# Last batch of an attention and gated-MLP kernel in chunks of 424, 424 and 240 columns, its gates in other buffers, and its keys in three stretches of matmuls per batch

## The chip, the cores and the metric

The kernel runs on one core of a Trainium2 chip. The core has a matmul engine (TensorE, in the profile PE, with the loads of its stationary operand listed apart as PEld), VectorE (DVE), ScalarE (ACT), GpSimd (POOL) and SyncE (SP), which issues the DMAs. Each engine works through its own list of instructions in order and waits on semaphores for the others. The metric is the time of one execution on the device in microseconds: the median of three runs of this kernel is 345.65 us (345.07 to 345.81).

## The reference

For each of four batches, linear attention with features that are outer products of two small projections, and then a gated MLP that mixes over the sequence:

```python
# q, k, v: (4, 4 heads, 1088, 32); S1, S2: (8, 32)
phi(x) = outer(S1 x, S2 x)                       # 64 features per head
kv = sum_s phi(k)_s v_s ;  z = sum_s phi(k)_s
x  = (phi(q) kv) / (phi(q) z + 1e-6)             # (4, 1088, 128)
h  = relu(x @ w_in)                              # (4, 1088, 1024)
u, v = h[..., :512], h[..., 512:]
v_n = (v - mean(v)) / sqrt(var(v) + 1e-6)
v_s = w_spatial @ v_n + b_spatial                # 1088 x 1088 over the sequence
out = (u * v_s) @ w_out                          # (4, 1088, 128)
```

The weights come in float64. The kernel splits them, and what it multiplies them with, into a high and a low fp32r part, and replaces a product by three (high by high, low by high, high by low).

## The kernel before, in words

A batch b has two halves. `attention(b)` makes x: queries, keys (`keys`), their products, and then `hidden_v`, which gives the normalised v half. `main(b)` does the rest with the sequence on the free axis. Its work is cut into blocks (d, c): d counts the four groups of 128 of the 512 hidden units, c the chunks of the 1088 output positions, which the table `CH` sets to 364, 362 and 362 columns. A block has

- `hidden(d, c)`: three matmuls (lines 357 to 359) into the bank `pu`, and a Relu on ACT (line 867) into a tile u,
- `spatial`: 26 matmuls over the nine pieces kt of the sequence into a bank `sp` (lines 875, 877, 884, 886),
- `gate`: DVE multiplies `sp` by u (line 913), ACT casts the product to its high part (line 437), DVE subtracts to get the low part (line 367),
- `out_mm`: three matmuls with w_out into a bank `po`, which collects over d. They are held back by one block in the list `late`.

After the last d a copy takes `po` to SBUF and a DMA takes it out. In the last batch the last block is cut in two, of 182 and 180 columns, and the sums of its chunk lie in two banks (`po` and `sd`) for all four d, so that each d there has six short out matmuls in place of three. One half is copied by DVE (line 857), the rest by ACT (line 855).

Tiles come from small rings: u from three buffers, which also serve the copies `ob`, the gates' parts from three buffers g (for the last d also r), attention's feature tiles from eight buffers pl, x in its parts from two buffers each, xh and xl.

Nobody writes the instructions' order down. Every step is recorded by `op` with an engine, a cost and a due time, and `Order.schedule` then walks through a modelled time: of what can start it takes what is due first, and fixes each engine's list and each tile's buffer. A changed cost or tile therefore can move instructions elsewhere.

In `keys(b)` for b over 0, three pieces g of the sequence are projected (`project`, 6 small matmuls a piece, line 531) and summed with v (`part`, 12 small matmuls a piece, line 579); the trace has two records for each of these. Here the matmuls are plain fp32 and 64 wide, and they stand in stretches between the fp32r matmuls of `main(b - 1)`: first the projection of piece 0, then twice a projection with the sums of the piece before, then the sums of the last piece.

Of the kernel before, what the change touches and what calls it, by code (L numbers as in the profile page):

```python
# [19 lines left out]
P = 128  # L20
# [5 lines left out]
CH = [(0, 364, 0), (364, 362, 1), (726, 362, 2), (726, 182, 2), (908, 180, 2)]  # L26
# [275 lines left out]
def c_dve(n):  # L302
    return 152 + 1.045 * n
# [10 lines left out]
def c_mm(n, k=1):  # L314
    return k * (n + 10.3) / 2.25
# [3 lines left out]
def tile_kernel(ctx: ExitStack, tc: tile.TileContext, kT, qT, vA, sks, idn, msk, wT, w_in, w_out, bsp, out):  # L319
# [166 lines left out]
    def load_w(kt, c):  # L486
        c0, cw, _ = CH[c]
# [36 lines left out]
    def ab_view(ab):  # L524
        return ab[:, :192].rearrange("p (x t c) -> p x t c", t=3, x=2)

    def project(ab, xt):

        for t in range(3):
            for j in range(2):  # L530
                nc.tensor.matmul(ab_view(ab)[64 * j:64 * j + 64, :, t], xt[:, t * P + 64 * j:t * P + 64 * j + 64], sk[:, :NSK], start=True, stop=True)  # L531

    def features(b, g, ab, what):

        a_sb = tl("ka", f"{what}a{b}{g}", [P, 3, 32])
        op("ACT", c_act(96, True), lambda: nc.scalar.copy(out=a_sb.ap, in_=ab_view(ab)[:, 0]), r=[ab], w=[a_sb])
        f = tl("kp", f"{what}p{b}{g}", [P, 3, H * R * R])
        if not b:
            op("DVE", c_dve(768), lambda: nc.vector.tensor_tensor(
                out=f.ap.rearrange("p t (h i j) -> p (t h) i j", h=H, i=R),  # L540
                in0=a_sb.ap.rearrange("p t (h i) -> p (t h) i", h=H).unsqueeze(3).broadcast_to([P, 12, R, R]),
                in1=ab_view(ab)[:, 1].rearrange("p t (h j) -> p (t h) j", h=H).unsqueeze(2).broadcast_to([P, 12, R, R]),
                op=ALU.mult,
            ), r=[a_sb, ab], w=[f])
            return f
        for a in range(2):
            op("DVE", c_dve(384), lambda a=a: nc.vector.tensor_tensor(
                out=f.ap.rearrange("p t (r i a j) -> p (t r) i a j", r=2, i=R, a=2)[:, :, :, a],
                in0=a_sb.ap.rearrange("p t (r a i) -> p (t r) a i", r=2, a=2)[:, :, a].unsqueeze(3).broadcast_to([P, 6, R, R]),
                in1=ab_view(ab)[:, 1].rearrange("p t (r a j) -> p (t r) a j", r=2, a=2)[:, :, a].unsqueeze(2).broadcast_to([P, 6, R, R]),  # L550
                op=ALU.mult,
            ), r=[a_sb, ab], w=[(f, a)])
        return f
# [6 lines left out]
    def keys(b):  # L560
# [9 lines left out]
        f = phi(b, 0, xts[0], "k")  # L570
# [13 lines left out]
        for g in range(3):  # L584
            if b and g < 2:

                ab = bank("sd", f"kab{b}{g + 1}")
                op("PE", 1510, lambda g=g, f=f, ab=ab: (project(ab, xts[g + 1]), part(g, f)), r=[f, vs[g], xts[g + 1], (sk, "x")], w=[kv, ab])
                f = features(b, g + 1, ab, "k")
            else:  # L590
                op("PE", 950, lambda g=g, f=f: part(g, f), r=[f, vs[g]], w=[kv])
                if g < 2:
                    f = phi(b, g + 1, xts[g + 1], "k")
# [174 lines left out]
    def main(b, st):  # L768
        po = [None] * 5
# [67 lines left out]
        def out_mm(d, c, gh, gl):  # L837
            c0, cw, _ = CH[c]
            if b == B - 1 and c == 2:

                for part in (3, 4):
                    out_part(d, part, gh, gl, CH[part][0] - c0)
            else:
                out_part(d, c, gh, gl, 0)

        def out_part(d, c, gh, gl, g0):
            c0, cw, _ = CH[c]
            if d == 0:
                po[c] = bank("sd" if c == 4 else "po", f"po{b}{c}")
            o = po[c]  # L850
            op("PE", c_mm(cw, 3), lambda: mm3(o[:, :cw], woh[:, d], wol[:, d], gh[:, g0:g0 + cw], gl[:, g0:g0 + cw], start=(d == 0), stop=(d == ND - 1)), r=[gh, gl, (woh, d // 2), (wol, d // 2)], w=[o], due=due(c_mm(cw, 3)))
            if d == ND - 1:
                ob = tl("u", f"ob{b}{c}", [P, CW])
                if c != 4:
                    op("ACT", c_act(cw, True), lambda: nc.scalar.copy(out=ob[:, :cw], in_=o[:, :cw]), r=[o], w=[ob], due=clock[0] + 8000)
                else:
                    op("DVE", c_dve(cw), lambda: nc.vector.tensor_copy(out=ob[:, :cw], in_=o[:, :cw]), r=[o], w=[ob], due=clock[0] + 8000)
                op("SP", 470, lambda: nc.sync.dma_start(out=out[b, :, c0:c0 + cw], in_=ob[:, :cw]), r=[ob], kb=181, due=clock[0] + 12000)

        def hidden(d, c, tag="pu"):  # L860
            c0, cw, _ = CH[c]
# [4 lines left out]
            u = tl("u", f"u{b}{d}{c}", [P, CW])  # L866
            op("ACT", c_act(cw, True), lambda: nc.scalar.activation(u[:, :cw], pu[:, :cw], AF.Relu), r=[pu], w=[u], lead=LEAD[0])  # L867
            return u

        def high(d, c, sp, kt):  # L870

            vh, vl, vx = hl[d]
            c0, cw, _ = CH[c]
# [35 lines left out]
        def gate(d, c, sp, u):  # L909
            cw = CH[c][1]  # L910
            tag = "r" if last(d) and c < 2 else "g"
            gh, gl = tl(tag, f"gh{b}{d}{c}", [P, CW], F32R), tl(tag, f"gl{b}{d}{c}", [P, CW], F32R)
            op("DVE", c_dve(cw), lambda: nc.vector.tensor_tensor(out=u[:, :cw], in0=sp[:, :cw], in1=u[:, :cw], op=ALU.mult), r=[sp], w=[u], lead=LEAD[1])  # L913
            split(lambda: gh[:, :cw], lambda: gl[:, :cw], lambda: u[:, :cw], cw, [u], [gh], [gl])
            return gh, gl
# [120 lines left out]
```

## Time and profile before

| | |
|---|---|
| median of three runs | 345.65 us |
| the profiled execution | 345.83 us, of which the profile's span is 344.1 us |
| PE busy | 336.0 us, 98% of the span |
| PEld, DVE, ACT, POOL busy | 323.0, 208.2, 160.0, 52.5 us |
| granted TensorE clock | 1.00 of 2.4 GHz over the whole span |
| chain of waits | PE 87%, DVE 5%, DMA 4% of the span |

Matmuls are pipelined: one starts long before the one ahead has ended, so their busy times overlap. What one costs in a row of them is the distance of two starts. The time between the span and the execution's own time, 345.83 less 344.1, is 1.73 us.

### The profile page before, as it was taken

How to read it: one execution, taken by the hardware profiler on the slowest of the kernel's cores; microseconds unless marked ns; L12 is line 12 of the kernel's file. 1: busy time of each engine (PE TensorE's matmuls, PEld its weight loads, DVE VectorE, ACT ScalarE, POOL GpSimd, SP SyncE). 2: the span in 40 equal slices, each digit the busy share in tenths (PEclk: the TensorE clock that was granted, in tenths of full speed). 3: DMA queues.
4: the chain of work that ended last, by engine and by line, in shares of the span. 5: the costliest groups of instructions: out<-in, count | busy, mean ns of one | idle time of the engine just before them, and what ended most of it. 6: DMA issues, size and time to landing. Idle time of an engine off the chain costs nothing.

```text
span 344.1 us, 6204 instructions
## 1 busy us (share of the span) xinstructions
PE 336.0 (98%) x2363; PEld 323.0 (94%) x2363; DVE 208.2 (61%) x480; ACT 160.0 (47%) x369; POOL 52.5 (15%) x66
## 2 busy tenths in 40 slices
PE   7889999999999999999999999999999999999995
PEld 7878999999999999999999999999999999999994
DVE  4799999833789993558995045235499941212122
ACT  2479746733667662445673153125666532112122
POOL 1030100352322034501300024302200000000000
PEclk9999999999999999999999999999999999999999
DMA  6556036865510056611000056400000010000001
GB/s 214 161 171 202 2 86 167 264 115 111 159 39 27 2 105 108 159 54 46 21 0 2 22 92 137 79 0 3 0 0 2 22 45 0 0 2 0 2 2 65
DMA packets 18502, 23.10 MB, mean 67 GB/s; under 512 B 2856, under 2 KB 17960, under 8 KB 18472
## 3 DMA queue, kind: packets, MB, share of 16 engines
q1 hardware_dynamic: 18472, 22.71, 26.0%
q8 instruction: 18, 0.29, 0.4%
q14 instruction: 12, 0.10, 0.1%
HBM read 13.78 MB, written 2.23 MB: 47 GB/s over the span
## 4 chain that ended last, share of the span: by engine, by line
PE 87%; DVE 5%; DMA 4%; ACT 1%; SPq 1%; issue 1%; DVEq 0%; ACTq 0%
PE sp L875 21%; PE sp L884 18%; PE sp L877 18%; PE sd L358 3%; PE sd L359 3%; PE sd L357 3%; PE pu L357 2%; PE pu L359 2%; PE pu L358 2%; PE sp L886 2%; PE po L357 2%; PE po L358 2%; PE po L359 2%; PE sd L579 2%; DMA c<-in_qT 1%; PE sd L531 1%
## 5 line engine op out<-in xcount | busy, mean ns | idle before, releaser
L875 PE MATMUL sp<-wTh,vh 128*128 128x362 f32 (+3 forms) x423 | 139.9, 331 | 0.0
L877 PE MATMUL sp<-wTh,vl 128*128 128x362 f32 (+3 forms) x376 | 122.6, 326 | 0.1
L884 PE MATMUL sp<-wTl,vh 128*128 128x362 f32 (+3 forms) x376 | 120.5, 326 | 0.0
L875 PEld LDWEIGHTS sp<-wTh,vh 128*128 128x128 f32 x423 | 79.6, 188 | 1.3
L877 PEld LDWEIGHTS sp<-wTh,vl 128*128 128x128 f32 x376 | 70.8, 188 | 1.0 <-DVE vl L824 0.6
L884 PEld LDWEIGHTS sp<-wTl,vh 128*128 128x128 f32 x376 | 70.8, 189 | 0.0
L913 DVE TENSOR_TENSOR u<-sp,u 128x362 f32<-128x362 f32 (+3 forms) x47 | 24.5, 523 | 71.9 <-PE sp L886 66.7
L437 ACT CAST g<-u 128x362 fp32r<-128x362 f32 (+3 forms) x47 | 23.0, 489 | 60.2 <-DVE u L913 60.2
L867 ACT ACTIVATE u<-pu 128x362 f32<-128x362 f32 (+3 forms) x49 | 22.9, 467 | 26.5 <-PE pu L359 26.2
L367 DVE TENSOR_TENSOR g<-u,g 128x362 fp32r<-128x362 f32 (+3 forms) x47 | 26.7, 569 | 13.3 <-ACT g L437 12.0
L740 DVE BATCH_NORM_STATS2 st<-vt 128x6 f32<-128x512 f32 x36 | 24.2, 686 | 9.1 <-ACT vt L738 8.9
L738 ACT ACTIVATE vt<-sd 128x512 f32<-128x512 f32 x36 | 21.3, 596 | 13.3 <-PE sd L359 12.6
L718 DVE RECIPROCAL c<-c 128x384 f32<-128x384 f32 (+1 forms) x9 | 21.8, 2418 | 8.1 <-ACT c L716 6.8
L370 POOL TENSOR_TENSOR r<-pl,r 128x384 fp32r<-128x384 f32 (+1 forms) x18 | 17.3, 969 | 43.6 <-ACT r L437 43.6
L687 POOL TENSOR_TENSOR pl<-pl,pl 128x384 f32<-128x384 f32 (+1 forms) x18 | 17.7, 982 | 36.1 <-DMA pl<-abT 26.4
L793 ACT CAST vh<-vt 128x384 fp32r<-128x384 f32 x36 | 17.8, 512 | 9.0 <-DVE vt L760 7.5
L370 POOL TENSOR_TENSOR r<-c,r 128x384 fp32r<-128x384 f32 (+1 forms) x9 | 9.4, 1061 | 77.8 <-ACT r L437 77.8
L795 DVE TENSOR_TENSOR vl<-vt,vh 128x384 fp32r<-128x384 f32 (+1 forms) x36 | 17.3, 504 | 0.8 <-ACT vh L793 0.6
L357 PE MATMUL pu<-xh,wih 128*128 128x362 f32 (+3 forms) x49 | 16.2, 331 | 0.0
L359 PE MATMUL pu<-xh,wil 128*128 128x362 f32 (+3 forms) x49 | 16.0, 327 | 0.0
L358 PE MATMUL pu<-xl,wih 128*128 128x362 f32 (+3 forms) x49 | 15.9, 324 | 0.0
L760 DVE TENSOR_SCALAR vt<-vt,mv,sm 128x512 f32<-128x512 f32 x31 | 15.5, 540 | 0.0
(147 smaller groups left out, 526.4 us busy)
## 6 DMA issues: line engine op xcount, KB each, us to landing
pl<-in_wT SPq DMA_DIRECT2D x18, 181.0 KB, 2.9
v<-in_vA SPq DMA_DIRECT2D x12, 198.0 KB, 4.0
kt<-in_kT SPq DMA_DIRECT2D x12, 192.0 KB, 3.8
pl<-abT SPq DMA_DIRECT2D x12, 192.0 KB, 4.0
c<-in_qT SPq DMA_DIRECT2D x9, 192.0 KB, 3.2
pl<-abT SPq DMA_DIRECT2D x24, 72.0 KB, 2.6
pl<-in_wT SPq DMA_DIRECT2D x9, 182.0 KB, 2.6
out<-u SPq DMA_DIRECT2D x7, 181.0 KB, 2.6
```

Of the source, the lines that this page charges most:

```text
L357: nc.tensor.matmul(o, ah, bh, start=start, stop=False)
L358: nc.tensor.matmul(o, ah, bl, start=False, stop=False)
L359: nc.tensor.matmul(o, al, bh, start=False, stop=stop)
L367: return lambda: nc.vector.tensor_tensor(out=o(), in0=a(), in1=bb(), op=ALU.subtract)
L370: return lambda: nc.gpsimd.tensor_tensor(out=o(), in0=a(), in1=bb(), op=ALU.subtract)
L437: op("ACT", c_act(n), lambda: nc.scalar.copy(out=hi(), in_=x()), r=r, w=wh)
L740: op("DVE", 690, lambda stats=stats, t=t: nc.vector.bn_stats(out=stats.ap, in_=vt[:, t]), r=[(vt, t)], w=[stats])
L867: op("ACT", c_act(cw, True), lambda: nc.scalar.activation(u[:, :cw], pu[:, :cw], AF.Relu), r=[pu], w=[u], lead=LEAD[0])
L875: nc.tensor.matmul(sp[:, :cw], vh[:, kt], wTh[:, kt, cs], start=(kt == 0), stop=False)
L877: nc.tensor.matmul(sp[:, :cw], vl[:, kt], wTh[:, kt, cs], start=False, stop=False)
L884: nc.tensor.matmul(sp[:, :cw], vh[:, kt], wTl[:, kt, cs], start=False, stop=False)
L913: op("DVE", c_dve(cw), lambda: nc.vector.tensor_tensor(out=u[:, :cw], in0=sp[:, :cw], in1=u[:, :cw], op=ALU.mult), r=[sp], w=[u], lead=LEA ...
```

## The change

Three things, all in the order of PE or at the end.

1. In the last batch the chunks are 424, 424 and 240 columns (`CH_LAST`), and no block is cut in two. The wide chunks take u and the copies `ob` from the ring pl, and both gate parts of chunk 0 share one buffer of the ring xh, of chunk 1 one of xl; each ring has one buffer to spare there, since the other holds the batch's x. In the last d the held-back out matmuls all come after the last block.
2. The last chunk's `po` is copied by halves, DVE the second and ACT the first.
3. `keys` of batches 1 to 3 projects pieces 0 and 1 together, then piece 2 with the sums of piece 0, and then sums pieces 1 and 2.

```diff
+CH_LAST = [(0, 424), (424, 424), (848, 240)]
...
-        for g in range(3):
-            if b and g < 2:
-                ab = bank("sd", f"kab{b}{g + 1}")
-                op("PE", 1510, lambda g=g, f=f, ab=ab: (project(ab, xts[g + 1]), part(g, f)), r=[f, vs[g], xts[g + 1], (sk, "x")], w=[kv, ab])
-                f = features(b, g + 1, ab, "k")
-            else:
...
+        ab = bank("sd", f"kab{b}0")
+        op("PE", 950, lambda ab=ab: (project(ab, xts[0]), project(ab, xts[1], 192)), r=[xts[0], xts[1], (sk, "x")], w=[ab])
+        f0, f1 = features(b, 0, ab, "k"), features(b, 1, ab, "k", 192)
+        ab = bank("sd", f"kab{b}2")
+        op("PE", 1305, lambda ab=ab: (project(ab, xts[2]), part(0, f0)), r=[f0, vs[0], xts[2], (sk, "x")], w=[kv, ab])
+        f2 = features(b, 2, ab, "k")
+        op("PE", 1660, lambda: (part(1, f1), part(2, f2)), r=[f1, f2, vs[1], vs[2]], w=[kv])
...
-                for part in (3, 4):
-                    out_part(d, part, gh, gl, CH[part][0] - c0)
...
-                ob = tl("u", f"ob{b}{c}", [P, CW])
-                if c != 4:
-                    op("ACT", c_act(cw, True), lambda: nc.scalar.copy(out=ob[:, :cw], in_=o[:, :cw]), r=[o], w=[ob], due=clock[0] + 8000)
-                else:
-                    op("DVE", c_dve(cw), lambda: nc.vector.tensor_copy(out=ob[:, :cw], in_=o[:, :cw]), r=[o], w=[ob], due=clock[0] + 8000)
+                ob = tl("pl" if wide else "u", f"ob{b}{c}", [P, cw])
+                n = cw
+                if wide and c == 2:
+                    n = cw // 2
+                    op("DVE", c_dve(n), lambda: nc.vector.tensor_copy(out=ob[:, n:], in_=o[:, n:cw]), r=[o], w=[(ob, 1)], due=clock[0] + 8000)
+                op("ACT", c_act(n, True), lambda: nc.scalar.copy(out=ob[:, :n], in_=o[:, :n]), r=[o], w=[(ob, 0)], due=clock[0] + 8000)
...
+            u = tl("pl" if wide and c < 2 else "u", f"u{b}{d}{c}", [P, cw])
...
-            tag = "r" if last(d) and c < 2 else "g"
+            if wide and c < 2:
+                g = tl(("xh", "xl")[c], f"g{b}{d}{c}", [P, 2, cw], F32R)
+                parts = [(lambda: g[:, 0], (g, 0)), (lambda: g[:, 1], (g, 1))]
+            else:
+                tag = "r" if last(d) else "g"
...
-            if late and not (last(d) and c):
+            if late and not last(d):
                 out_mm(*late.pop(0))
...
-        if b == B - 1:
-            blocks[-1:] = [(ND - 1, 3), (ND - 1, 4)]
```

The first place is PE's list in batch 1's keys, at the last of their stretches, before; `kp` holds features, `sd_117` the sums, `sp` the mixing of batch 0.

```order
L875 MATMUL sp_290<-wTh,vh 128x362
L877 MATMUL sp_290<-wTh,vl 128x362
L884 MATMUL sp_290<-wTl,vh 128x362
L579 MATMUL sd_117<-v_113,kp_134 64x66 x12
L875 MATMUL sp_290<-wTh,vh 128x362
L877 MATMUL sp_290<-wTh,vl 128x362
```

The same place of PE's list after the change, where lines are shifted by one or so.

```order
L876 MATMUL sp_290<-wTh,vl 128x362
L883 MATMUL sp_290<-wTl,vh 128x362
L579 MATMUL sd_117<-v_109,kp_138 64x66 x12
L579 MATMUL sd_117<-v_113,kp_134 64x66 x12
L874 MATMUL sp_290<-wTh,vh 128x362
L876 MATMUL sp_290<-wTh,vl 128x362
```

The sums of piece 1 (`kp_138`), which stood behind a projection twelve rows earlier, now stand beside those of piece 2, and the projection of piece 1 stands beside that of piece 0 in the same way; a stretch is gone.

The second place is the end of PE's list before: the out matmuls behind the last matmul of the last block, with the semaphores that each waits for.

```order
L886 MATMUL sp_252<-wTl,v_85 128x180
L357 MATMUL po_266<-r_788,woh 128x364
L358 MATMUL po_266<-r_800,woh 128x364
L359 MATMUL po_266<-r_788,wol 128x364
L357 MATMUL po_115<-r_776,woh 128x362 [waits Activation_49]
L358 MATMUL po_115<-r_786,woh 128x362 [waits DVE_49]
L359 MATMUL po_115<-r_776,wol 128x362
L357 MATMUL po_237<-g_674,woh 128x182 [waits Activation_49]
L358 MATMUL po_237<-g_640,woh 128x182 [waits DVE_49]
L359 MATMUL po_237<-g_674,wol 128x182
L357 MATMUL sd_117<-g_650,woh 128x180 [waits Activation_49]
L358 MATMUL sd_117<-g_640,woh 128x180 [waits DVE_49]
```

The same after the change, from the first out matmul behind the last block (whose last matmul has 240 columns) to the end of the list.

```order
L358 MATMUL po_237<-g_650,woh 128x240
L359 MATMUL po_237<-g_640,woh 128x240
L360 MATMUL po_237<-g_650,wol 128x240
L358 MATMUL po_266<-xh_309,woh 128x424
L359 MATMUL po_266<-xh_309,woh 128x424 [waits DVE_49]
L360 MATMUL po_266<-xh_309,wol 128x424
L358 MATMUL po_115<-xl_319,woh 128x424 [waits Activation_49]
L359 MATMUL po_115<-xl_319,woh 128x424 [waits DVE_49]
L360 MATMUL po_115<-xl_319,wol 128x424
L358 MATMUL po_237<-r_788,woh 128x240 [waits Activation_49]
L359 MATMUL po_237<-r_800,woh 128x240 [waits DVE_49]
L360 MATMUL po_237<-r_788,wol 128x240
```

Twelve out matmuls follow the last block in both, but now the first three are the third group's on the last chunk (`g_650`, `g_640`), the next six are wide, and the last two parts (`r_788`, `r_800`) have buffers of their own, while before the last low part went into `g_640`, which the three matmuls ahead of it read.

The third place is the end of ACT's list before.

```order
L437 CAST g_650<-u_679 128x180 [waits DVE_49]
L855 COPY u_609<-po_266 128x364 [waits PE_49,Activation_49]
L855 COPY u_635<-po_115 128x362 [waits PE_49,Activation_49]
L855 COPY u_679<-po_237 128x182 [waits DVE_49,PE_49]
L1032 UNCONDITIONAL_BRANCH
```

And after the change; DVE's last row there is its own copy of the other half of `po_237`, which waits for PE.

```order
L438 CAST r_788<-u_635 128x240 [waits DVE_49]
L856 COPY pl_191<-po_266 128x424 [waits PE_49]
L856 COPY pl_63<-po_115 128x424 [waits PE_49]
L856 COPY pl_212<-po_237 128x120 [waits DVE_49]
L1036 UNCONDITIONAL_BRANCH
```

The last copy on ACT now waits for DVE alone and not for PE, that is for DVE's copy of the other half of the same bank; no copy waits for a DMA any more, since the buffers pl are free.

## Rows read from the trace of the kernel before

**Rows 1.** The page: busy time by engine, and the granted clock in 40 slices.
```profile
PE 336.0 (98%) x2363; PEld 323.0 (94%) x2363; DVE 208.2 (61%) x480; ACT 160.0 (47%) x369; POOL 52.5 (15%) x66
PEclk9999999999999999999999999999999999999999
```

**Rows 2.** Windows, last batch: PE, PEld, DVE, ACT, POOL busy, clock, DMA.
```profile
280.00:325.00 45.00, 45.00 (x276) 45.00 (x276) 9.13 (x17) 8.62 (x18) 0.00 (x0) 1.00 0.01 5
```

**Rows 3.** Waits of PE from 40 us to the end: total, times, longest.
```profile
PE sd L358 <- DVE g L367: 0.3, 1, 0.3
```

**Rows 4.** Timeline of PE (start, us, ...): 26 of 364 columns, 6 of 512.
```profile
289.32 0.33 PE L357 MATMUL pu<-xh,wih 128*128 128x364 f32 x1
...
293.65 0.25 PE L357 MATMUL po<-g,woh 128*128 128x182 f32 x1
...
242.41 0.40 PE L357 MATMUL sd<-wih,xh 128*128 128x512 f32 x1
...
243.81 0.33 PE L875 MATMUL sp<-wTh,vh 128*128 128x362 f32 x1
```

**Rows 5.** Timeline of PE: 182 columns behind wide ones, 16 steps of 180.
```profile
325.99 0.25 PE L357 MATMUL po<-g,woh 128*128 128x182 f32 x1
326.07 0.28 PE L358 MATMUL po<-g,woh 128*128 128x182 f32 x1
...
336.02 0.27 PE L875 MATMUL sp<-wTh,vh 128*128 128x180 f32 x1
...
337.81 0.27 PE L886 MATMUL sp<-wTl,v 66*128 66x180 f32 x1
```

**Rows 6.** Groups of DVE and ACT from 325 us on: busy us, mean ns, idle before.
```profile
L913 DVE TENSOR_TENSOR u<-sp,u 128x364 f32<-128x364 f32 x1 | 0.5, 536 | 4.0 <-PE sp L886 4.0
...
L437 ACT CAST r<-u 128x364 fp32r<-128x364 f32 x1 | 0.5, 497 | 4.4 <-DVE u L913 4.4
...
L855 ACT COPY u<-po 128x364 f32<-128x364 f32 x1 | 0.5, 455 | 0.0
...
L855 ACT COPY u<-po 128x182 f32<-128x182 f32 x1 | 0.3, 311 | 0.2 <-DVE g L367 0.2
```

**Rows 7.** Timeline of PE: last matmul ahead, second behind, three stretches of batch 3.
```profile
204.97 0.33 PE L359 MATMUL pu<-xh,wil 128*128 128x362 f32 x1
...
205.99 0.33 PE L877 MATMUL sp<-wTh,vl 128*128 128x362 f32 x1
...
209.70 0.32 PE L884 MATMUL sp<-wTl,vh 128*128 128x362 f32 x1
...
211.43 0.33 PE L877 MATMUL sp<-wTh,vl 128*128 128x362 f32 x1
...
222.62 0.32 PE L884 MATMUL sp<-wTl,vh 128*128 128x362 f32 x1
...
224.00 0.32 PE L877 MATMUL sp<-wTh,vl 128*128 128x362 f32 x1
```

**Rows 8.** Line 547, products of features: ns min/median/max, first and last start.
```profile
L547 DVE TENSOR_TENSOR kp<-ka,sd x18: 541/548/556, 67.0 to 216.0; 128x384 f32<-128x384 f32 x18
```

**Rows 9.** Timeline behind the last block; in brackets idle time before, releaser.
```profile
338.12 0.35 DVE L913 TENSOR_TENSOR u<-sp,u 128x180 f32<-128x180 f32 x1 [1.12 <-PE sp L886]
...
338.50 0.34 ACT L437 CAST g<-u 128x180 fp32r<-128x180 f32 x1 [1.88 <-DVE u L913]
...
339.41 0.35 DVE L367 TENSOR_TENSOR g<-u,g 128x180 fp32r<-128x180 f32 x1 [0.94 <-PE po L359]
...
340.00 0.27 PE L359 MATMUL sd<-g,wol 128*128 128x180 f32 x1
341.22 0.35 DVE L857 COPY u<-sd 128x180 f32<-128x180 f32 x1 [1.46 <-DMA out<-u]
```

**Rows 10.** DMA issues by size: KB each, median us from issue to landing.
```profile
out<-u SPq DMA_DIRECT2D x4, 182.0 KB, 1.9
...
out<-u SPq DMA_DIRECT2D x1, 91.0 KB, 1.9
```

More of the change, by code (lines that the diff above doesn't have):

```diff
@@ L486, in load_w @@
     def load_w(kt, c):
-        c0, cw, _ = CH[c]
+        c0, cw = CH[c]
         cs = slice(c0, c0 + cw)
@@ L521, in load_sq, with ab_view, project, features @@
         split(lambda: sqh.ap, lambda: sql.ap, lambda: sq[:, :P], P, [sq], [sqh], [sql])
-    def ab_view(ab):
-        return ab[:, :192].rearrange("p (x t c) -> p x t c", t=3, x=2)
-    def project(ab, xt):
+    def ab_view(ab, at=0):
+        return ab[:, at:at + 192].rearrange("p (x t c) -> p x t c", t=3, x=2)
+    def project(ab, xt, at=0):
         for t in range(3):
             for j in range(2):
-                nc.tensor.matmul(ab_view(ab)[64 * j:64 * j + 64, :, t], xt[:, t * P + 64 * j:t * P + 64 * j + 64], sk[:, :NSK], start=True, stop=True)
-    def features(b, g, ab, what):
+                nc.tensor.matmul(ab_view(ab, at)[64 * j:64 * j + 64, :, t], xt[:, t * P + 64 * j:t * P + 64 * j + 64], sk[:, :NSK], start=True, stop=True)
+    def features(b, g, ab, what, at=0):
         a_sb = tl("ka", f"{what}a{b}{g}", [P, 3, 32])
-        op("ACT", c_act(96, True), lambda: nc.scalar.copy(out=a_sb.ap, in_=ab_view(ab)[:, 0]), r=[ab], w=[a_sb])
+        op("ACT", c_act(96, True), lambda: nc.scalar.copy(out=a_sb.ap, in_=ab_view(ab, at)[:, 0]), r=[ab], w=[a_sb])
         f = tl("kp", f"{what}p{b}{g}", [P, 3, H * R * R])
@@ L582, in part @@
                         )
[L584 to L593 removed]
+        if not b:
+            for g in range(3):
+                f = phi(b, g, xts[g], "k")
+                op("PE", 950, lambda g=g, f=f: part(g, f), r=[f, vs[g]], w=[kv])
+            return kv
+        ab = bank("sd", f"kab{b}0")
[5 more added lines that the diff above has]
+        op("PE", 1660, lambda: (part(1, f1), part(2, f2)), r=[f1, f2, vs[1], vs[2]], w=[kv])
         return kv
@@ L768, in main @@
     def main(b, st):
-        po = [None] * 5
+        po = [None] * 3
+        cols = CH_LAST if b == B - 1 else CH
+        wide = b == B - 1
         clock, rate = [T_MAIN[b] * 1e3], [1.0]
@@ L835, in split_t, with out_mm @@
                 op("DVE", c_dve(DH), low9(nc.vector), r=[(vt, t)], w=[(h, kt) for h in hs], sh=True, alts=[("POOL", c_pool(DH), low9(nc.gpsimd))], kind="vl0")
[L837 to L847 removed]
+        def out_mm(d, c, hi, lo, parts):
+            c0, cw = cols[c]
@@ L848, in out_part @@
             if d == 0:
-                po[c] = bank("sd" if c == 4 else "po", f"po{b}{c}")
+                po[c] = bank("po", f"po{b}{c}")
             o = po[c]
-            op("PE", c_mm(cw, 3), lambda: mm3(o[:, :cw], woh[:, d], wol[:, d], gh[:, g0:g0 + cw], gl[:, g0:g0 + cw], start=(d == 0), stop=(d == ND - 1)), r=[gh, gl, (woh, d // 2), (wol, d // 2)], w=[o], due=due(c_mm(cw, 3)))
+            op("PE", c_mm(cw, 3), lambda: mm3(o[:, :cw], woh[:, d], wol[:, d], hi(), lo(), start=(d == 0), stop=(d == ND - 1)), r=[*parts, (woh, d // 2), (wol, d // 2)], w=[o], due=due(c_mm(cw, 3)))
@@ new lines, in out_mm @@
+                n = cw
[3 more added lines that the diff above has]
+                op("ACT", c_act(n, True), lambda: nc.scalar.copy(out=ob[:, :n], in_=o[:, :n]), r=[o], w=[(ob, 0)], due=clock[0] + 8000)
+                op("SP", 470, lambda: nc.sync.dma_start(out=out[b, :, c0:c0 + cw], in_=ob.ap), r=[ob], kb=cw // 2, due=clock[0] + 12000)
@@ L889, in spatial @@
             vh, vl, vx = hl[d]
-            _, cw, wc = CH[c]
+            c0, cw = cols[c]
+            wcs = [n for n, (w0, w) in enumerate(CH) if w0 < c0 + cw and c0 < w0 + w]
             g = kt // 3
@@ L895, in spatial @@
             if high in parts:
-                r += ([(vl, key)] if kt < NK else []) + [(wTh, (kt, wc))]
+                r += ([(vl, key)] if kt < NK else []) + [(wTh, (kt, wc)) for wc in wcs]
             if low in parts:
-                r += [(wTl, (kt, wc))] + ([(wTl, ("bias", 0)), (wTl, ("bias", 1)), vx] if kt == NK else [])
+                r += [(wTl, (kt, wc)) for wc in wcs] + ([(wTl, ("bias", 0)), (wTl, ("bias", 1)), vx] if kt == NK else [])
             def f():
@@ L909, in gate @@
         def gate(d, c, sp, u):
-            cw = CH[c][1]
-            tag = "r" if last(d) and c < 2 else "g"
[L912 to L915, printed above, removed]
+            cw = cols[c][1]
+            op("DVE", c_dve(cw), lambda: nc.vector.tensor_tensor(out=u.ap, in0=sp[:, :cw], in1=u.ap, op=ALU.mult), r=[sp], w=[u], lead=LEAD[1])
+            if wide and c < 2:
[3 more added lines that the diff above has]
+                tag = "r" if last(d) else "g"
+                gh, gl = tl(tag, f"gh{b}{d}{c}", [P, cw], F32R), tl(tag, f"gl{b}{d}{c}", [P, cw], F32R)
+                parts = [(lambda: gh.ap, gh), (lambda: gl.ap, gl)]
+            (hi, wh), (lo, wl) = parts
+            split(hi, lo, lambda: u.ap, cw, [u], [wh], [wl])
+            return hi, lo, [wh, wl]
         late = []
```

20 lines of the change are left out of this document (8 added, 12 removed).

## The prediction

> **What bounds the kernel now.** I read the page first: TensorE is busy for 98% of the span, at a granted clock of 1.00 throughout (the 2.4 GHz level), and no other engine above 61% [rows 1]. Then the busy time by stretches: in the last batch TensorE is busy for all 45.00 us of the window from 280 to 325 us, its weight loads too [rows 2]. Then TensorE's waits: behind the first 40 us there is one, of 0.3 us, at the very end [rows 3]. So the time is the sum of TensorE's steps plus what follows its last one, and it is no use to look at the other engines before the end. A busy time of overlapping matmuls says nothing of their price, so the timeline gives that as distances of starts. 26 matmuls of 364 columns take 293.65 - 289.32 = 4.33 us, 0.1665 each; six of 512 take 1.40 us, 0.2333 each [rows 4]. In a row of short ones, 16 steps of 180 columns take 1.79 us, 0.112 each; but the one 182-column step that follows wide matmuls takes 0.08 [rows 5]. So 182 columns stream in 0.08, and a row of them is held at 0.112 by something else; every matmul has a weight load of its own, 276 of each in that window [rows 2], so I take the loads as that floor.
>
> **Last batch: 41 matmuls fewer.** Up to the last matmul of the last block (the tail behind it comes below) the last batch had 125 matmuls of 364 and 212 of 362 columns and 76 short ones: twelve blocks of 29, the last one done twice on halves, and three out matmuls per block (six on the cut chunk) less the twelve of the tail. At 0.1665 and 0.112 that is 56.11 + 8.51 = 64.62 us. Now it is 250 of 424 and 122 of 240. The trace has neither width. For 424 I go along the line between 364 and 512 columns, 0.00045 us a column: 0.1665 + 60 x 0.00045 = 0.1936; the two rows also bound it, at 0.1665 and 0.2333, but a line through them has held at both. For 240 the same line gives 0.111 and the floor of the short ones 0.112; the far bounds are the 0.08 of a lone short step and the 0.1665 of 364 columns. I take 0.112, the nearest row, and keep 0.118 for the range, in case load and stream disturb each other where they are equal. Sum: 48.40 + 13.66 = 62.06 us, that is **2.6 us less** (1.8 with 0.118). In words: the 76 short matmuls each paid 0.03 us for a load that was longer than their stream, and they go.
>
> On the price of a step: the Trainium skill (TensorE: Matmul & The Clock Gate, Back-to-back issue gap) gives columns over 2.4 plus 2.5 ns for an isolated matmul, 154 ns for 364 columns where this trace has 166.5; the measurement decides. By that rule 424 columns would cost 179 ns, and with the same page's 106.7 ns for a 128-column weight load (LDWEIGHTS) as the floor the term would be some 2.3 us in place of 2.6, an estimate.
>
> **Gates and copies off the end.** The wide gates in xh and xl and the u tiles in pl sit on DVE, ACT and the rings. In the last batch DVE is busy for 9.13 of 45 us and ACT for 8.62 [rows 2], so longer instructions there are hidden behind TensorE. A gate's chain on 424 columns, some 0.6 + 0.55 + 0.6 us by the rows of 364 [rows 6], must end before the out matmuls that read it, which stand most of a block (3 to 5 us) behind. I cost them at nothing; without that cover each would cost its 1.7 us.
>
> **Keys: one stretch fewer in three batches.** A stretch of small fp32 matmuls costs more than its contents, because the switch into it and out of it shows. From the start of the last wide matmul ahead to the second start behind, less two wide steps (0.333): projection alone 1.02 - 0.33 = 0.69; projection and sums 1.73 - 0.33 = 1.40; sums alone 1.38 - 0.33 = 1.05 [rows 7]. Alone they make 1.74, together 1.40: a stretch costs 0.34 us by itself. Each of the three batches had four stretches and has three with the same contents: 3 x 0.34 = **1.0 us less**. The bounds are nothing, if the 0.34 belongs to the kind of matmul, and 1.0; since the joined stretch in the trace saves it although it joins two kinds, I take all of it. What could take its place is a wait for the features of piece 2: their buffer comes free only with the sums of piece 0, now in the same stretch. Between the two stretches of batch 1 stand twelve wide matmuls, 2.0 us, and the two feature products there take 1.1 us on DVE [rows 8], so 0.5 us or more is left, and piece 1's sums come first.
>
> **The tail.** Before: the last block's last matmul starts at 337.81 [rows 5], the span ends at 344.1: 6.29 us. In it the low part waits for a buffer (339.41, released by the out matmuls, though the cast is done at 338.84), and the last copy for the landing of an earlier output DMA, 1.46 us of idle time [rows 9]. Both waits go. After, counted from that last matmul's start T: DVE's product of 240 columns starts at T + 0.33 (0.31 before, and 60 columns more) and takes 0.346 + 60 x 0.00104 = 0.41, the cast 0.39, the subtraction 0.41 (on the line between 180 and 364 columns, [rows 6, 9]), with gaps of 0.03, the one between product and cast: ready at T + 1.60. TensorE meanwhile does the nine other out matmuls, 0.112 + 3 x 0.112 + 6 x 0.1936 = 1.61, and one of the last three; the second starts at T + 1.72, so the gate is hidden by some 0.1. The last one starts at T + 1.83 and ends 0.30 later. Then DVE's half copy of 120 columns, 0.28, and ACT's, 0.26 (from 0.311 for 182 and 0.455 for 364, [rows 6]), one behind the other, since ACT waits for DVE in the new order: with gaps T + 2.73. From the end of the last copy to the end of the span it was 341.57 to 344.1, 2.53 us. An output of 182 KB lands as fast as one of 91, in 1.9 us [rows 10], so size costs nothing; for two 212 KB outputs just ahead I add 0.1 (bounds 0 and 0.4). The tail is 5.36 us, **0.9 less** (0.6 to 1.1).
>
> That the two halves follow each other is what the lists show. The Trainium skill (PSUM — Partial Sum Buffer, PSUM bank collisions raise a hardware error) says that ScalarE and VectorE must not read one bank and quadrant at once, even at other columns, so they need a semaphore between them. No run here has shown it yet. Side by side they would take 0.28 us in place of 0.57, and the tail would be at most 0.3 shorter.
>
> **Sum.** 2.6 + 1.0 + 0.9 = 4.5 us, from the profiled execution's 345.83: **341.3 us**. That execution is 0.18 above the median of the runs shown, inside their own spread of 0.74, so I leave it.
>
> **Rivals.** *The stretch is not what costs.* If the 0.34 us goes with each kind of small matmul, the keys give nothing: 342.3. For it: the long steps at a stretch's ends could be waits for the last small product; against it, joining has saved it twice per batch already. *New waits of TensorE in batches 1 to 3.* The order of queries, hidden rows and gates moved in batch 1; before there was no wait, since the planner left room, and its room is the same now; two or three waits of 0.5 us would give 342.3 to 343. *Narrow matmuls pay by the column.* If 0.112 for 180 columns is a rate, 240 cost 0.149, 122 + 6 of them 4.7 us more: 346.0, no change. The 0.08 for 182 columns speaks against it. *One gate buffer per chunk, the slower side.* The cast of a wide gate must wait until the out matmuls of the group before have read the buffer, and those out matmuls are held back by a block. Were they so late that the next gate's cast and subtraction (1.15 us) stood in front of TensorE in each of three groups on two chunks, 6.9 us would come on: 348.2; it decides from 0.86 us per time on, 5.2 us over six. Against it: in the new lists these out matmuls stand a block or more ahead of the gate that overwrites them.
>
> **How the numbers follow.** Forecast 0.72, on its own 340.7 to 342.0; stretches 0.10; new waits 0.10; rate by the column 0.03; gate buffers 0.03; the rest, spread out, 0.02. The range of 340.6 to 342.9 holds the forecast, the stretches and most of the waits. What the measurement can tell from no change is about 0.2%, 0.7 us: faster 0.95, same 0.03, slower 0.02.
>
> **What would show it.** Starts 0.194 apart at 424 columns and 0.111 to 0.112 at 240, with nothing shorter left; three stretches of small matmuls per batch, 1.0, 1.4 and 1.75 us by the reckoning above; no wait of TensorE behind 40 us but perhaps one below 0.1 us at the last low part; the last copies one behind the other without a DMA ahead of them, and 5.4 us from the last block's last matmul to the end. Wrong it would be by steps of 0.12 or more at 240 columns, by a TensorE wait at a `pu`, `sp` or key stretch, or by an output DMA that lands later than 2 us.

## The result, and the profile after the change

The changed kernel takes 342.21 us against 345.62 us for the kernel before on the same chip: ratio 0.9898, 95% interval 0.9881 to 0.9915. One of its executions, the one profiled with that timing, was slow (346.81 us, with a granted clock of 0.55 and 0.69 between 17 and 35 us), and the ratio leaves it out. Timed a second time, as the first experiment below, the changed kernel gives 342.03 against 345.74 us, 0.9899 (0.9881 to 0.9917). The forecast was 341.3 us: the direction and the three mechanisms hold, and the time is 0.7 to 0.9 us above it. That lies just outside the 340.7 to 342.0 that the forecast gave itself and close to the 342.3 of two rivals, so the time alone does not tell them apart; the experiments do.

All rows of the changed kernel are from the profile of that second timing, whose span is 340.51 us against 344.05. Its page, busy time by engine and the granted clock in 40 slices; compare [rows 1].

```profile
PE 333.4 (98%) x2322; PEld 319.7 (94%) x2322; DVE 206.9 (61%) x478; ACT 160.2 (47%) x367; POOL 52.7 (15%) x66
PEclk9999999999999999999999999999999999999999
```

There are 41 matmuls fewer, and nothing else of note on the page: the bound is the same engine at the same clock. The list of PE's waits behind 40 us is now empty, where [rows 3] had one. So, as before, the steps of PE tell the story.

The last batch in PE's timeline (start, us, engine, line, tile): the first matmul of a row of 240 columns, the first of the row of 424 behind it, and the first of the next row.

```profile
317.40 0.27 PE L358 MATMUL pu<-xh,wih 128*128 128x240 f32 x1
...
319.98 0.36 PE L358 MATMUL po<-xl,woh 128*128 128x424 f32 x1
...
331.42 0.27 PE L874 MATMUL sp<-wTh,vh 128*128 128x240 f32 x1
```

23 matmuls of 240 columns take 319.98 - 317.40 = 2.58 us, 0.1122 each, and 59 of 424 take 11.44 us, 0.1939 each. The prediction had 0.112 and 0.1936.

The three key stretches of batch 3, each by the last wide matmul ahead and the second behind, as in [rows 7].

```profile
204.82 0.33 PE L360 MATMUL pu<-xh,wil 128*128 128x362 f32 x1
...
206.20 0.33 PE L876 MATMUL sp<-wTh,vl 128*128 128x362 f32 x1
...
212.27 0.33 PE L883 MATMUL sp<-wTl,vh 128*128 128x364 f32 x1
...
214.00 0.33 PE L359 MATMUL pu<-xl,wih 128*128 128x364 f32 x1
...
220.49 0.33 PE L883 MATMUL sp<-wTl,vh 128*128 128x362 f32 x1
...
222.58 0.33 PE L876 MATMUL sp<-wTh,vl 128*128 128x362 f32 x1
```

Less two wide steps each (0.333), that is 1.05, 1.40 and 1.76 us, 4.21 in all; the four stretches of before make 0.69 + 2 x 1.40 + 1.05 = 4.54. A stretch less is worth 0.33 us, and 0.34 was expected.

The end, on PE, DVE and ACT; in brackets the idle time before and what ended it. Compare [rows 9].

```profile
334.95 0.28 PE L885 MATMUL sp<-wTl,v 66*128 66x240 f32 x1
...
335.26 0.41 DVE L911 TENSOR_TENSOR u<-sp,u 128x240 f32<-128x240 f32 x1 [0.72 <-PE sp L885]
...
335.71 0.40 ACT L438 CAST r<-u 128x240 fp32r<-128x240 f32 x1 [1.79 <-DVE u L911]
...
336.13 0.41 DVE L368 TENSOR_TENSOR r<-u,r 128x240 fp32r<-128x240 f32 x1 [0.46 <-ACT r L438]
...
336.81 0.27 PE L360 MATMUL po<-r,wol 128*128 128x240 f32 x1
337.12 0.28 DVE L855 COPY pl<-po 128x120 f32<-128x120 f32 x1 [0.58 <-PE po L360]
337.44 0.26 ACT L856 COPY pl<-po 128x120 f32<-128x120 f32 x1 [0.17 <-DVE pl L855]
```

Counted from the last block's last matmul, everything up to the last copy's end runs as forecast: product, cast and low part hidden, the copies one behind the other, and no engine waits for a DMA. The last copy ends at 337.70, 2.75 us behind that matmul (2.73 forecast). But the span ends at 340.51, 2.81 us later, and not 2.63. So the tail, from that matmul's start to the end of the span, is 5.56 us where 5.36 was expected and 6.24 were before (the prediction has 6.29, from the span as rounded to 344.1).

What the DMA engines do there, by windows of half a microsecond (columns as in [rows 2], the last two being the DMA engines' busy share and GB/s).

```profile
337.50:338.00 0.50, 0.00 (x0) 0.00 (x0) 0.00 (x0) 0.20 (x1) 0.00 (x0) 1.00 0.87 305
338.00:338.50 0.50, 0.00 (x0) 0.00 (x0) 0.00 (x0) 0.00 (x0) 0.00 (x0) 1.00 1.03 363
338.50:339.00 0.50, 0.00 (x0) 0.00 (x0) 0.00 (x0) 0.00 (x0) 0.00 (x0) 1.00 0.98 352
339.00:339.50 0.50, 0.00 (x0) 0.00 (x0) 0.00 (x0) 0.00 (x0) 0.00 (x0) 1.00 0.29 94
```

And in the kernel before, while its last output, of 90 KB, goes out alone.

```profile
342.10:342.60 0.50, 0.00 (x0) 0.00 (x0) 0.00 (x0) 0.00 (x0) 0.00 (x0) 1.00 0.29 91
342.60:343.10 0.50, 0.00 (x0) 0.00 (x0) 0.00 (x0) 0.00 (x0) 0.00 (x0) 1.00 0.32 94
```

After the change three outputs of 212, 212 and 120 KB go out at once and fill all 16 DMA engines at some 360 GB/s; the last output, which used to travel alone, now queues behind the other two. The Trainium skill (DMA: Bandwidth & Descriptors, Specifications) gives some 358 GB/s as the limit of HBM per core; the 352 and 363 here agree with it, though no run here shows what sets them.

To compare two executions I count from the start of the first key stretch of batch 1, since the time ahead of it varies between executions (it is 66.08, 65.83 and 65.24 us in three kernels that are alike up to there, e1, e5 and e8 below). From that point to the last block's last matmul it is 337.81 - 65.89 = 271.92 us before and 334.95 - 66.08 = 268.87 after, 3.05 less; with the tail, 0.68 less, the change is worth 3.73 us from there on. The profile of the first timing, with 70.58 us ahead of that point, has 274.45 us behind it, and e1 has 274.43.

How much of the 3.05 us is the last batch's can be read from the matmul behind the last 512-column one, before and after.

```profile
265.19 0.33 PE L875 MATMUL sp<-wTh,vh 128*128 128x362 f32 x1
```

```profile
264.28 0.33 PE L874 MATMUL sp<-wTh,vh 128*128 128x362 f32 x1
```

From there to the last block's last matmul stand 461 steps and 72.62 us before, 423 steps and 70.67 us after. Three of the steps after are 362-column ones of the batch before, which stood ahead of that point before the change (0.50 us). So the last batch itself is 72.62 - 70.67 + 0.50 = 2.45 us shorter, for 41 matmuls fewer, and the other 0.60 us are the keys' and whatever else changed up to there.

### The profile page after: what moved, and what is told of

The parts are those of the page before. It is cut to its first block, busy times and chain, and to the rows that moved or that the text cites. A ratio compares the mean times of both kernels' runs of the same rounds, so it can differ in the third digit from the quotient of the medians.

```text
span 345.0 us, 6124 instructions
## 1 busy us (share of the span) xinstructions
PE 337.4 (98%) x2322; PEld 324.3 (94%) x2322; DVE 206.3 (60%) x478; ACT 159.9 (46%) x367; POOL 52.2 (15%) x66
## 4 chain that ended last, share of the span: by engine, by line
PE 91%; DMA 3%; DVE 2%; ACT 2%; SPq 1%; issue 0%; ACTq 0%
PE sp L874 20%; PE sp L883 18%; PE sp L876 17%; PE sd L358 4%; PE sd L359 4%; PE sd L360 4%; PE pu L358 3%; PE po L358 2%; PE po L359 2%; PE pu L360 2%; PE po L360 2%; PE pu L359 2%; PE sp L885 2%; PE sd L579 2%; PE sp L644 1%; DMA c<-in_qT 1%
## 5 line engine op out<-in xcount | busy, mean ns | idle before, releaser
L874 PE MATMUL sp<-wTh,vh 128*128 128x362 f32 (+3 forms) x414 | 137.4, 332 | 0.0
L876 PE MATMUL sp<-wTh,vl 128*128 128x362 f32 (+3 forms) x368 | 120.9, 329 | 0.1
L883 PE MATMUL sp<-wTl,vh 128*128 128x362 f32 (+3 forms) x368 | 118.8, 328 | 0.0
L874 PEld LDWEIGHTS sp<-wTh,vh 128*128 128x128 f32 x414 | 77.9, 188 | 1.2
L876 PEld LDWEIGHTS sp<-wTh,vl 128*128 128x128 f32 x368 | 69.2, 188 | 1.1 <-DVE vl L830 0.3
L911 DVE TENSOR_TENSOR u<-sp,u 128x362 f32<-128x362 f32 (+2 forms) x38 | 19.6, 517 | 41.7 <-PE sp L885 38.8
L438 ACT CAST g<-u 128x362 fp32r<-128x362 f32 (+2 forms) x39 | 19.0, 488 | 35.0 <-DVE u L911 34.7
L368 DVE TENSOR_TENSOR g<-u,g 128x362 fp32r<-128x362 f32 (+2 forms) x39 | 23.1, 592 | 8.9 <-ACT g L438 8.5
L866 ACT ACTIVATE u<-pu 128x362 f32<-128x362 f32 (+2 forms) x40 | 18.5, 464 | 20.6 <-PE pu L360 20.4
L911 DVE TENSOR_TENSOR pl<-sp,pl 128x424 f32<-128x424 f32 x8 | 4.8, 600 | 33.2 <-PE sp L885 31.6
```

Source lines behind the costliest of these rows:

```text
L368: return lambda: nc.vector.tensor_tensor(out=o(), in0=a(), in1=bb(), op=ALU.subtract)
L874: nc.tensor.matmul(sp[:, :cw], vh[:, kt], wTh[:, kt, cs], start=(kt == 0), stop=False)
L876: nc.tensor.matmul(sp[:, :cw], vl[:, kt], wTh[:, kt, cs], start=False, stop=False)
L883: nc.tensor.matmul(sp[:, :cw], vh[:, kt], wTl[:, kt, cs], start=False, stop=False)
L911: op("DVE", c_dve(cw), lambda: nc.vector.tensor_tensor(out=u.ap, in0=sp[:, :cw], in1=u.ap, op=ALU.mult), r=[sp], w=[u], lead=LEAD[1])
```

## The experiments

Times are medians; "before" is the kernel before, timed beside it on the same chip. "From the stretch" is the time from the start of the first key stretch in batch 1 to the end of the span; where that stretch was moved, there is none. "Tail" is the time from the start of the last block's last matmul to the end of the span.

| kernel | us | before | ratio (95%) | span | from the stretch | tail |
|---|---|---|---|---|---|---|
| before | | | | 344.05 | 278.16 | 6.24 |
| e1 the change again | 342.03 | 345.74 | 0.9899 (0.9881 to 0.9917) | 340.51 | 274.43 | 5.56 |
| e2 keys alone | 345.25 | 345.74 | 0.9985 (0.9975 to 0.9994) | 343.83 | 277.54 | 6.23 |
| e3 last batch alone | 342.45 | 345.74 | 0.9910 (0.9899 to 0.9922) | 341.49 | 275.16 | 5.54 |
| e4 chunks 364, 362, 362 | 342.43 | 345.74 | 0.9902 (0.9888 to 0.9917) | 340.58 | 274.93 | 6.20 |
| e5 one copy (single run) | 342.07 | 345.67 | | 340.26 | 274.43 | 5.57 |
| e6 chunks 448, 448, 192 | 344.47 | 345.67 | 0.9961 (0.9948 to 0.9974) | 342.70 | 276.73 | 5.64 |
| e7 keys in two stretches | 341.31 | 345.67 | 0.9874 (0.9859 to 0.9889) | 339.53 | | 5.55 |
| e8 small outputs (single run) | 341.23 | 345.67 | | 339.43 | 274.19 | 5.39 |
| e9 e7, outputs swapped | 341.22 | 345.82 | 0.9873 (0.9858 to 0.9888) | 339.50 | | 5.38 |
| e10 before, copies in pl | 344.95 | 345.82 | 0.9978 (0.9969 to 0.9987) | 342.99 | 277.42 | 5.45 |

**e1, the changed kernel again.**

> The changed kernel once more, unchanged, for a second profiled execution and more times. Theory A (the three terms of the prediction, two of them smaller than predicted: last batch's stream 2.2 us less, keys 1.0 less, tail 0.75 less): some 341.9 us beside 345.6 of the kernel before, starts 0.194 us apart at 424 columns and 0.112 at 240, no wait of TensorE behind 40 us, 2.8 us from the end of the last copy to the end of the span. Theory B (the terms were right at 4.5 us and something else took 1 us, a new wait in batches 1 to 3): waits of TensorE of together about 1 us behind 50 us.

It gives 342.03 us, and its profile is the one shown above.

**e2, the new keys in the kernel before; e3, the changed kernel with the old keys.** The edit of e2 is the part of the diff in `keys`; e3 is the changed kernel without it.

> The kernel before with the keys of the changed one (three stretches) and nothing else. Theory A (a stretch costs 0.34 us by itself): 1.0 us less than before, 344.6; joined projections 0.85 us from first to following start, joined sums 1.56, against 0.50 and 0.86 for one alone; the last copy still idle for 1.4 us behind an output DMA. Rival (the cost belongs to each kind of small matmul): 345.6, as before.

> The changed kernel with the keys as before (four stretches). Theory A: 1.0 us more than the changed kernel, 343.0, so 2.7 us less than before. Rival (keys give nothing): as the changed kernel, 342. If the two parts are not independent (the planner's order moves), e2 and e3 will not add up to the whole.

From the stretch to the last block's last matmul, e2 takes 271.31 us and e3 269.62, 0.61 and 2.30 less than before; together 2.91, and both at once give 3.05. e2's tail is that of before, e3's that of the change. So the parts nearly add up (most of the 0.14 between is late steps of e3's own order, named below), and the keys bring 0.6 and not 1.0. The medians, 0.5 for e2 and 0.4 between e3 and e1, can't be told from that. Ahead of the stretch e2 has a wait that is not in before. PE's waits in e2 (total, times, longest):

```profile
PE sd L358 <- POOL r L370: 0.6, 1, 0.6
```

It stands at 63.25 us, in batch 1's queries; the profile of the whole change has none there. The missing 0.3 us of the keys are waits of another kind, in the weight loads. Two rows of that view from e1, and the longer of the two in PE's timeline:

```profile
PEld sd L358 <- issue: 0.3, 1, 0.3
...
PEld sd L358 <- ACT vt L741: 0.2, 1, 0.2
```

```profile
110.80 0.32 PE L883 MATMUL sp<-wTl,vh 128*128 128x362 f32 x1
111.14 0.47 PE L358 MATMUL sd<-wih,xh 128*128 128x512 f32 x1
111.44 0.39 PE L359 MATMUL sd<-wil,xh 128*128 128x512 f32 x1
```

From 110.80 to 111.14 stands 0.34 us in place of 0.167, and the next step is 0.30 in place of 0.233: 0.24 us lost. The other place, at 100.48, loses 0.11. In batch 1 of e2 the same two places lose 0.34 us in all; in the kernel before one such step is late, by 0.05, and in e3 two steps lose 0.15. So with the new keys PE loses some 0.3 us in batch 1's hidden rows (`hidden_v`), and shows it as late weight loads although the list of its own waits is empty. For the shorter place the view names what came last, ACT's work on an earlier hidden row (`vt`); for the longer one it names nothing (issue), so what was late there stays open.

**e4, no 424-column chunks: the last batch in 364, 362 and 362 columns, uncut.**

```diff
-CH_LAST = [(0, 424), (424, 424), (848, 240)]
+CH_LAST = [(0, 364), (364, 362), (726, 362)]
```

> The changed kernel with chunks of 364, 362 and 362 columns in the last batch, uncut, everything else as changed. Theory A (what the last batch saves is the 41 matmuls whose weight load is longer than their stream, not the width): the stream up to the last block's last matmul is as long within 0.2 us, the tail 0.5 us longer, since the last chunk's gate (1.7 us after its product starts) now ends after the nine other out matmuls (1.67 us) and copies are 60 columns longer: 342.3. Rival (the wide chunks as such are cheaper per column): 343.5 or more.

From the stretch to the last block's last matmul it is 334.38 - 65.65 = 268.73 us, within 0.14 of e1's 268.87. So the gain in the stream is the 41 matmuls that are gone, and not the width of those that stay. The tail is 6.20 us against 5.56: the last gate's chain works on 362 columns in place of 240, its low part is ready at 336.45, and PE waits for it.

```profile
336.03 0.33 PE L358 MATMUL po<-r,woh 128*128 128x362 f32 x1
...
336.50 0.43 PE L359 MATMUL po<-r,woh 128*128 128x362 f32 x1
```

That second step is 0.47 us behind the first, 0.167 without a wait. What the narrow last chunk is for is this chain. By the medians e4 is 0.4 us behind e1, less than the two intervals can part.

**e5, one copy: ACT copies all 240 columns of the last chunk.**

```diff
-                if wide and c == 2:
+                if False:
```

> The changed kernel with the last chunk's copy by ACT alone, all 240 columns. If the two halves truly run one behind the other (0.28 and 0.26 us and a gap), one copy of 0.36 us ends 0.2 us earlier behind the last matmul, and so does the span. Rival (the halves overlap in effect, or their order is hidden): one copy ends no earlier.

The one copy:

```profile
336.91 0.37 ACT L856 COPY pl<-po 128x240 f32<-128x240 f32 x1
```

It ends 2.59 us behind the last block's last matmul (334.69), 0.16 sooner than the second half did, and still the tail is 5.57 us against 5.56: no difference. The windows of its end (columns as above) say why.

```profile
337.30:337.80 0.50, 0.00 (x0) 0.00 (x0) 0.00 (x0) 0.00 (x0) 0.00 (x0) 1.00 0.96 339
337.80:338.30 0.50, 0.00 (x0) 0.00 (x0) 0.00 (x0) 0.00 (x0) 0.00 (x0) 1.00 1.02 360
338.30:338.80 0.50, 0.00 (x0) 0.00 (x0) 0.00 (x0) 0.00 (x0) 0.00 (x0) 1.00 1.00 357
```

The DMA engines are full until 338.8. A last copy that ends earlier or later by 0.1 to 0.2 us only changes how long its output queues. The copy on two engines therefore buys nothing here.

**e6, the price of a narrow step: chunks of 448, 448 and 192 columns.**

```diff
-CH_LAST = [(0, 424), (424, 424), (848, 240)]
+CH_LAST = [(0, 448), (448, 448), (896, 192)]
```

> The changed kernel with last-batch chunks of 448, 448 and 192 columns. Theory A (a matmul's step is its stream, but not under the 0.112 us of its weight load): 192 columns stay at 0.112 where 240 are, and 448 cost 0.204 in place of 0.194: 256 times 0.0107 is 2.7 us more than the changed kernel, 344.7. Rival (short matmuls pay by the column): 192 columns at 0.09, the gain of 128 steps at 0.022 cancels it: 342.

In PE's timeline, the first two matmuls of a row of 23 at 192 columns, of 59 at 448, and the first of the next row:

```profile
318.99 0.25 PE L358 MATMUL pu<-xh,wih 128*128 128x192 f32 x1
319.08 0.27 PE L359 MATMUL pu<-xl,wih 128*128 128x192 f32 x1
...
321.53 0.39 PE L358 MATMUL po<-xl,woh 128*128 128x448 f32 x1
321.76 0.37 PE L359 MATMUL po<-xl,woh 128*128 128x448 f32 x1
...
333.55 0.25 PE L874 MATMUL sp<-wTh,vh 128*128 128x192 f32 x1
```

0.1104 each at 192 columns and 0.2037 at 448. Of the 23, the first takes 0.09 us and the others 0.111 each, and the first wide one behind takes 0.23 in place of 0.20. A fifth fewer columns (192 in place of 240) save next to nothing in a row, while the wide ones pay for theirs; the kernel is 2.4 us slower than e1. A row of narrow steps has a floor near 0.11 us, and 240 columns stand just on it.

**e7, keys in two stretches.** All three pieces are projected together, and all three summed together; the features of piece 2 go into the tiles of its keys, which have been read by then.

```diff
-        ab = bank("sd", f"kab{b}0")
-        op("PE", 950, lambda ab=ab: (project(ab, xts[0]), project(ab, xts[1], 192)), r=[xts[0], xts[1], (sk, "x")], w=[ab])
+        ab, ab2 = bank("sd", f"kab{b}0"), bank("sd", f"kab{b}2")
+        op("PE", 1390, lambda ab=ab, ab2=ab2: (project(ab, xts[0]), project(ab, xts[1], 192), project(ab2, xts[2])), r=[xts[0], xts[1], xts[2], (sk, "x")], w=[ab, ab2])
...
+        features(b, 2, ab2, "k", into=xts)
+        op("PE", 2440, lambda: (part(0, f0), part(1, f1), part(2, xts)), r=[f0, f1, *xts, vs[0], vs[1], vs[2]], w=[kv])
```

> The changed kernel with keys in two stretches per batch: all three projections, then all sums (the third piece's features lie in the buffers of the projected keys, made by six short DVE products). Theory A (a stretch costs 0.34 us by itself): another 3 times 0.34, 1.0 us less than the changed kernel, 341.0, less what small new waits of TensorE give back. Rival (what is saved by joining is only the switch between a projection and sums): no change.

The two stretches of batch 1 in PE's timeline, each by the matmul ahead and the second behind:

```profile
73.45 0.32 PE L891 MATMUL sp<-wTl,vh 128*128 128x362 f32 x1
...
75.17 0.32 PE L359 MATMUL pu<-xl,wih 128*128 128x362 f32 x1
...
78.79 0.32 PE L891 MATMUL sp<-wTl,vh 128*128 128x362 f32 x1
...
81.58 0.33 PE L893 MATMUL sp<-wTl,v 66*128 66x362 f32 x1
```

By the same reckoning 1.39 and 2.46 us, 3.85 against e1's 4.21 in batch 3: once more 0.36 us per stretch, 1.1 over three batches. The time falls by 0.7, to 341.31 us; the order moves again and brings a new wait (PE's waits of e7):

```profile
PE po L359 <- DVE g L368: 0.2, 1, 0.2
```

The step there, from 124.62 us, takes 0.58 in place of 0.167, and a 512-column step at 112.17 takes 0.49 in place of 0.233. The kernel is 1.26% below before. Against the change, the medians are 0.7 us apart, and the two intervals overlap by a little; e9, the same keys once more, gives 341.22.

**e8, the outputs' share: of the last batch's two wide chunks only 32 columns are written out, the rest is left out.**

```diff
-                op("SP", 470, lambda: nc.sync.dma_start(out=out[b, :, c0:c0 + cw], in_=ob.ap), ...)
+                ... if not (wide and c < 2) else op("SP", 470, lambda: nc.sync.dma_start(out=out[b, :, c0:c0 + 32], in_=ob[:, :32]), ...)
```

> The changed kernel with only 32 of the 424 columns written out in the two wide chunks of the last batch (the other columns of these chunks are left out of the output). From the end of the last copy to the end of the span the changed kernel takes 2.8 us, the kernel before 2.5. If the large outputs just ahead hold up the last one: 2.5. If it is the last output's own size (120 KB beside 90) or the end of the program: 2.8 still.

The tail is 339.43 - 334.04 = 5.39 us, 0.17 shorter than e1's with all engines' work the same, and 5.36 was the forecast. (Its span is 1.08 us shorter than e1's, but 0.84 of that stands ahead of the first key stretch.) From the last copy's end it is 2.64 us, between the 2.48 of before and the 2.81 of e1. The DMA issues (KB each, median us to landing):

```profile
out<-pl SPq DMA_DIRECT2D x1, 120.0 KB, 1.7
out<-pl SPq DMA_DIRECT2D x2, 16.0 KB, 1.4
```

So 0.17 of the 0.20 us which the tail came out too long are the queue of 544 KB before the DMA engines: the last output lands 1.7 us after its issue here, and 1.9 in e1. The 0.16 us that stay above the 2.48 of before are not that queue; whether they are the last output's own 120 KB in place of 90, no run tells.

**e9, the wide outputs first: e7 with the last chunk's held-back products of the third group third in place of first.** (The expectation calls them the middle chunk's; in PE's list they have 240 columns.)

```diff
+        if wide:
+            late[:] = [late[1], late[2], late[0], late[3]]
```

> The kernel with keys in two stretches per batch, with the four output products of the last batch's end in another order: that of the middle chunk which came first now comes third, so that one wide product is ready 0.34 us earlier. Theory (the end is set by 544 KB of outputs going through the DMA engines at some 360 GB/s): an earlier first output brings the end forward by as much as its copy can begin earlier, up to 0.2 us, to 341.1 to 341.3. Rival (ScalarE's copies begin no earlier, since the gate's cast ends there last): no change against the kernel with two stretches, 341.3.

341.22 against e7's 341.31 us: the two can't be told apart by their times. In the profiles the tail is 5.38 us against 5.55 in e7, and ACT's first wide copy starts 1.06 us behind the last block's last matmul where it started 1.23 behind. That is the direction and the size that the theory has, 0.17 for 0.17, but in one profile each, and the times are 0.1 us apart, too little to settle it.

**e10, the DMA wait alone: the kernel before with the last batch's copies `ob` in the ring pl.**

```diff
-                ob = tl("u", f"ob{b}{c}", [P, CW])
+                ob = tl("pl" if b == B - 1 else "u", f"ob{b}{c}", [P, CW])
```

> The kernel before, with only one thing changed: the output tiles of the last batch lie in buffers that nothing else uses at that time, so that the last copy of a chunk waits for no earlier output's transfer. TensorE's order is that of before. Theory (the wait of the last copy for a transfer cost about 0.9 us): the copy begins as the last output product ends, near 340.3 instead of 341.2, its transfer starts when the three outputs ahead of it (454 KB at some 360 GB/s) are through, and the time falls by 0.6 to 0.9 us, to 344.8 to 345.1. Rival (the outputs ahead keep the DMA engines busy, so that the wait hid nothing): no change, 345.6.

The last copy in its timeline, and the DMA engines behind it by windows:

```profile
340.04 0.35 DVE L857 COPY pl<-sd 128x180 f32<-128x180 f32 x1 [0.55 <-PE sd L359]
```

```profile
340.50:341.00 0.50, 0.00 (x0) 0.00 (x0) 0.00 (x0) 0.00 (x0) 0.00 (x0) 1.00 1.00 337
341.00:341.50 0.50, 0.00 (x0) 0.00 (x0) 0.00 (x0) 0.00 (x0) 0.00 (x0) 1.00 0.66 197
```

PE ends the wait where [rows 9] had a DMA. From the last block's last matmul (337.54) to the end of the span it is 5.45 us against 6.24: the wait for the transfer was worth 0.79 us, and the time falls by 0.87, 0.22%. That is no less than the whole change gains in the tail (0.68), with one edited line, and the wait for the low part is still there. Without that wait the changed kernel's last copy ends 0.1 us sooner behind the last block's last matmul (2.75 against 2.85), but what follows the copy takes 2.81 us against 2.60, with the larger outputs ahead.

## Why the prediction came out as it did

**Last batch's steps: -2.6 forecast, -2.45 measured.** This term held within 0.15 us. The new steps have the price that was given them: 0.1937 at 424 columns and 0.1123 over all 122 at 240, 62.13 us in place of 62.06. The old ones come to the 64.6 us of the prediction within 0.1, though not step by step. It gave each of the 76 short ones 0.112. They stand in many rows, and [rows 5] shows that the first short step behind wide ones takes 0.08. What [rows 5] does not show is the first wide step behind a row of three that begins at 325.99:

```profile
326.30 0.35 PE L875 MATMUL sp<-wTh,vh 128*128 128x362 f32 x1
326.49 0.32 PE L877 MATMUL sp<-wTh,vl 128*128 128x362 f32 x1
```

The three short steps take 0.31 us and not 0.336, but the wide one behind takes 0.19 and not 0.1665. Together that is 0.50 us, what the flat prices give. Over the last batch before, the nine such first short steps average 0.085 and the eight wide ones behind a row 0.194: what the one saves, the other pays back. So the flat price was right for the sum; that it does not show which steps pay did no harm here. (The sentence on the Trainium skill's formula has a wrong sum: by its own figures the term would be 2.1 us and not 2.3. Nothing else rests on it.)

**Keys: -1.0 forecast, -0.6 measured.** The price of a stretch holds (0.33 and, in e7, 0.36 for 0.34), so the rival that the stretch isn't what costs is out. What failed is "before there was no wait, since the planner left room, and its room is the same now": the rival of new waits was true in part, 0.3 to 0.4 us of it, in the hidden rows of batch 1, and e2 has it with the keys alone. This is the largest part of what did not come.

**Tail: -0.9 forecast, -0.68 measured.** Each step up to the last copy came to a few hundredths. The term that was too small is "for two 212 KB outputs just ahead I add 0.1 (bounds 0 and 0.4)": it is 0.3, and in e8, with little ahead of the last output, 0.17 of it is gone. "An output of 182 KB lands as fast as one of 91" [rows 10] was misread. Those outputs did not travel apart: the copy for the 91 KB ended at 340.16, when the DMA engines had just begun on the 182 and 181 KB of the other two chunks, and they were full:

```profile
340.60:341.10 0.50, 0.00 (x0) 0.00 (x0) 0.00 (x0) 0.00 (x0) 0.00 (x0) 1.00 0.97 336
```

So its 1.9 us held a queue already; in e8, with little ahead of it, an output of 120 KB lands in 1.7 us and one of 16 KB in 1.4. Of the two waits that go, the one for the DMA is by far the larger (e10). That the copies follow each other was right; that side by side they would save 0.3 is not so here, since e5 shows the end to be the DMA engines'.

**The other rivals.** Narrow matmuls do not pay by the column (e6: 0.110 at 192, 0.112 at 240). One gate buffer per chunk brings no wait: no step of the last batch up to the tail is more than 0.03 us late. The three errors have one direction, 0.1 + 0.4 + 0.2 us, and make up most of the 0.7 to 0.9 us between forecast and measurement; the rest is no more than what the time ahead of the first key stretch varies by. That the weight loads are what makes the floor is argued from their number and not shown: no kernel here ran narrow matmuls without them.

## What to carry to other kernels

Where one engine is the bound, count its instructions in rows, and price a row of short ones together with the first long one behind it: what the first short one saves, that long one pays back. Removing short ones saves what they paid above their own columns, and here it did not matter how wide the others became (e4). Before you split the last copy, look at the windows of the DMA engines behind it: if they are full, free an output's buffer or send earlier outputs sooner. A change of order in a planned kernel gives back a part of its gain in small waits elsewhere, and on TensorE these can show in the weight loads alone.

## What the runs showed of the hardware

- A stretch of fp32 matmuls 64 wide between wide fp32r ones costs 0.33 to 0.36 us besides its contents.
- Rows of fp32r matmuls, each with its own weight load: 0.112 us a step at 180 columns, 0.110 at 192, 0.112 at 240, 0.167 at 364, 0.194 at 424, 0.204 at 448. The first of a row of 182 columns behind wide ones takes 0.08, and the first wide one (362) behind that row 0.19.
- Three outputs of 544 KB in all fill the 16 DMA engines for 1.6 us at some 360 GB/s; an output of 16 KB lands 1.4 us after its issue, one of 212 KB in 1.9.
